# Folding the last two quarters of w_in through sums and differences of the weights' halves

## The chip, the cores and the metric

The kernel runs on one core of a Trainium2 chip. The metric is the device time of one execution in microseconds; lower is better. The engines are TensorE (PE, with its weight loads shown as PEld), VectorE (DVE), ScalarE (ACT), GpSimd (POOL) and the SyncE queue (SP), which issues all DMAs here.

## The reference

The input `x` is 8 batches of 3008 x 256 fp32. The reference takes the real part of a 2-D FFT over both axes of each batch, and sends the 24064 resulting rows through a feed-forward layer:

```
X = fft(fft(x, axis=1), axis=2).real          # rows of 256
h = X @ w_in                                  # w_in: 256 x 2048
g = h if h >= 1; 0 if h <= -1; else (h + 1)**2 / 4
out = g @ w_out                               # w_out: 2048 x 256
```

The weights arrive as 64-bit floats.

## The kernel before

The FFT over the 256 columns is never computed on the data. It is a matrix of cosines and sines, and is multiplied into `w_in` once ("the fold"). So the kernel has two kinds of work: the FFT over 3008 rows (as 47 x 64, two stages of fp32 matmuls, per batch), and for every unit two matrix products with a nonlinearity between.

**Units.** A unit is one batch, one chunk of up to 512 output columns (three chunks a batch) and one block of 128 of the 2048 hidden features. `gemm1` (G) makes two products u and v, each of three fp32r matmuls (high and low halves of the operands). VectorE makes `us` (U) and then both sums in `h` (H), ScalarE `a` (R, Q), VectorE the larger of both (L), ScalarE the high half `gh` (J), GpSimd the two low halves `gl` (T, t). `gemm2` (M) multiplies by `w_out`, twelve matmuls, four units behind G. The tile `h` has three buffers, so H of a unit needs GpSimd to be done with t of the unit three before; `uv` has three banks of PSUM, shared with the folds of quarters 2 and 3.

**Weights.** `w_in` and `w_out` come in sixteen jobs of 128 x 512 values. Jobs 8 and 9 are the upper and lower half (rows 0 to 127 and 128 to 255) of quarter 2 of `w_in`, 12 and 13 those of quarter 3. Step l loads a job's 64-bit words into a raw tile on SP, e and v turn them into fp32 on ScalarE and VectorE (v's last instruction is L238). The two halves of a quarter share a pair tile (`cv_8`, `cv_12`). From job 8 on, raw tiles and pair tiles lie in the four buffers of the tag `xt`, in which also the first four `x` tiles of batches 1 and on lie (steps X). A buffer goes to a new tile when every instruction that touches the old one has been done.

**The fold.** Step a (cosines) or b (sines) of a quarter multiplies the constant matrices `mats[m][h]` with the two fp32 halves and adds both products in one PSUM bank: `out = sum over h of mats[m][h].T @ half[h]`. An fp32 matmul leaves two records in the trace. Then a.1 and b.1 take the high part to `wh` on ScalarE (b.1 first copies row 0, which is sent by two DMAs to `delta`), a.2 and b.2 the low part to `wl` on VectorE, and b.2 clears row 0 with two GpSimd memsets.

**Order.** For the first batch and part of the second the order of PE, ACT, DVE and POOL is written out by hand in WRITTEN: each engine takes its own instructions in that order. SP is not in it. In WRITTEN, y1 adds the two halves of x tile 1 of batch 1 (loaded by X1) on GpSimd; its place is behind t17 and ahead of the clearing of b3.2, T18, t18, T19 and y0.

Of the kernel before, what the change touches and what calls it, by code (L numbers as in the profile page):

```python
# [9 lines left out]
F32 = mybir.dt.float32  # L10
# [3 lines left out]
ALU = mybir.AluOpType  # L14
# [8 lines left out]
NA, NBB, NC = 64, 47, 24  # L23
P = 128
XC = 8
GPC = 4
KT = 3
XW = KT * P
CH = 512
# [5 lines left out]
C_ORDER = [*range(1, 8), 0, *range(8, NC)]  # L35
WIDTH = [7 * NA + 34, CH, CH]

G_ORDER = np.arange(P).reshape(XC, GPC, 2, 2).transpose(0, 3, 1, 2).reshape(-1)


SPANS = [(k * P // NBB * 2 * NC, (min((k + 1) * P, 8 * NBB) - 1) // NBB * 2 * NC + 2 * NC) for k in range(KT)]
# [3 lines left out]
def _constants():  # L45
# [7 lines left out]
    rm = np.block([[co, si], [-si, co]])  # L53
    ang = 2 * np.pi * (np.outer(k, G_ORDER) % D) / D
    mc, ms = np.cos(ang), np.sin(ang)
# [22 lines left out]
t2 M2 G6.1 G7 o6 J4 p12.1 T3 l8 t3 M3 T4 t4 o6.1 H5 R5 l9 Q5 p12.2 G7.1 H6 G8 U7 G8.1 R6 e7 Q6 L5 J5 T5 t5 H7  # L78
R7 v7 o7 L6 U8 M4 p13 o7.1 M5 Q7 p13.1 p13.2 L7 J6 J7 T6 t6 T7 t7 H8 p14 p14.1 G9 G9.1 G10 U9 H9 G10.1 U10
p14.2 R8 Q8 R9 Q9 e8 H10 L8 L9 J8 T8 R10 M6 G11 M7 G11.1 G12 M7.1 U11 M7.2 v8 U12 G12.1 M7.3 M7.4 Q10 J9 t8 M8  # L80
e9 H11 L10 J10 G13 U13 G13.1 T9 t9 H12 M9 T10 t10 v9 H13 R11 R12 Q11 Q12 L11 L12 R13 G14 U14 b2 G14.1 M10 G15
J11 T11 t11 Q13 L13 M11 J12 b2.1 T12 t12 H14 U15 b2.2 l10 G15.1 G16 R14 J13 l13 Q14 T13 t13 H15 a2 G16.1 L14
U16 H16 a2.1 R15 J14 M12 Q15 L15 a2.2 R16 J15 e12 Q16 T14 t14 G17 U17 G17.1 H17 R17 Q17 M13 v12 e13 G18 X0 U18
G18.1 G19 T15 t15 L16 H18 R18 v13 X1 L17 M14 M15 M15.1 J16 T16 Q18 t16 U19 M15.2 b3 L18 G19.1 G20 M15.3 H19
M15.4 M16 J17 T17 t17 y1 J18 b3.1 b3.2 U20 G20.1 G21 a3 H20 G21.1 R19 Q19 L19 U21 M17 T18 t18 H21 X3 G22 G22.1
M18 R20 J19 Q20 L20 R21 a3.1 U22 a3.2 G23 J20 Q21 l11 T19 y0 t19 H22 T20 t20 X2 y2 G23.1 l15 G24 M19 M20 U23
L21 H23 e11 R22 J21 Q22 T21 t21 v11 R23 o11 Q23 G24.1 o11.1 l14 L22 J22 T22 t22 q0 G25 q0.1 U24 H24 G25.1 R24
G26 Q24 U25 e10 L23 J23 H25 M21 G26.1 G27 L24 v10 J24 R25 T23 t23 o10 e14 M22 M23 o10.1 T24 t24 Q25 U26 G27.1
# [19 lines left out]
N_EARLY = 8  # L108
# [20 lines left out]
def fft_ffn_kernel(ctx: ExitStack, tc: tile.TileContext, x, cst, w_in, w_out, out):  # L129
    nc = tc.nc  # L130
# [14 lines left out]
    def fold_x(b, q):  # L145

        t = xt.pop((b, q))
        if b or q:
            y = sb.tile([P, XW], F32, tag="y", name=f"y_{b}_{q}", bufs=3) if b else t[:, 0]
            nc.gpsimd.tensor_tensor(y, t[:, 0], t[:, 1], op=ALU.add)  # L150
            yt[b, q] = [y]
        else:
            yt[b, q] = [t[:, 0], t[:, 1]]
        if q == 0:
            y = sb.tile([P, NA], F32, tag="yd", name=f"yd_{b}", bufs=1)
            nc.gpsimd.tensor_tensor(y, t[:, 0, :NA], t[:, 1, :NA], op=ALU.subtract)
            yt[b, "d"] = y
# [5 lines left out]
    mats = [[cm[:, (2 * m + h) * P : (2 * m + h + 1) * P] for h in range(2)] for m in range(2)]  # L163
# [14 lines left out]
    def fft_bank(b, name):  # L178

        if b == 0 and early[0] < EARLY_BANKS:  # L180
            early[0] += 1
            return ps.tile([P, CH], F32, tag=f"acc{early[0] % 4}", name=name, bufs=1)
        return ps.tile([P, CH], F32, tag="fft", name=name, bufs=1)

    def split(hi, lo, src, eng=nc.vector):
        nc.scalar.activation(hi, src, AF.Copy)
        yield
        eng.tensor_tensor(lo, src, hi.bitcast(F32), op=ALU.subtract)  # L188
# [2 lines left out]
    jobs = []  # L191
    for f4 in range(4):
        jobs += [("in", f4, 0), ("in", f4, 1), ("out", 2 * f4), ("out", 2 * f4 + 1)]
    raws, mags, f32s, drows = {}, {}, {}, {}

    def load_w(n):
        if n >= len(jobs):
# [29 lines left out]

    def assemble(n):
        raw, t = raws.pop(n), mags.pop(n)
        low, high = raw[:, :, 0], raw[:, :, 1]  # L230
        bits = t.bitcast(U32)
        if n in VECTOR_LOWS:
            nc.vector.tensor_scalar(low, low, 2.0**-29, 7.0, op0=ALU.mult, op1=ALU.min)
        nc.vector.scalar_tensor_tensor(bits, bits, 3, low, op0=ALU.logical_shift_left, op1=ALU.bitwise_or)
        if n not in f32s:
            f32s[n] = low.bitcast(F32)
        w = f32s[n].bitcast(U32)
        nc.vector.scalar_tensor_tensor(w, high, 0x80000000, bits, op0=ALU.bitwise_and, op1=ALU.bitwise_or)  # L238
# [13 lines left out]
    def fold_bank(f4, name):  # L252
        if f4 < 2:
            return fft_bank(0, name)
        return ps.tile([P, CH], F32, tag="uv", name=name, bufs=3)

    def fold_w_in(f4, m):
        cols = slice(f4 * CH, (f4 + 1) * CH)
        pt = fold_bank(f4, f"wps_{f4}_{m}")
        for h in range(2):  # L260
            nc.tensor.matmul(pt, mats[m][h], f32s[4 * f4 + h], start=(h == 0), stop=(h == 1))  # L261
        yield
        if m == 0:
            yield from split(wh[m][:, cols], wl[m][:, cols], pt)
            return
        t = sb.tile([P, CH], F32, tag="us", name=f"drow_{f4}", bufs=2)[:1]
        nc.scalar.activation(t, pt[:1, :], AF.Copy)
        drows[f4] = t
        if f4:
            row = dr.tile([1, CH], F32, tag="drow", name=f"drow_{f4}", bufs=2)  # L270
            nc.sync.dma_start(row, t)
            nc.sync.dma_start(delta[:, f4 * 4 : f4 * 4 + 4], row.rearrange("o (i p) -> p (o i)", p=P))
        yield from split(wh[m][:, cols], wl[m][:, cols], pt)
        if f4:
            clear_row(f4)

    def clear_row(f4):
        for w in (wh, wl):
            nc.gpsimd.memset(w[1][:1, f4 * CH : (f4 + 1) * CH].bitcast(F32), 0.0)

    def first_delta():
        t = drows[0]
        pt = fft_bank(0, "dps")[:, : 4 * NA].rearrange("p (i n) -> p i n", i=4)
        for i in range(4):
            nc.tensor.matmul(pt[:, i], t[:, i * P : (i + 1) * P], half[:1].to_broadcast([1, NA]), start=True, stop=True)
        yield
        nc.scalar.activation(delta[:, :4], pt[:, :, 0], AF.Copy, scale=2.0)

    def stage1(b, q):
        for p in range(q, min(q + 2, XC)):  # L290
            if b > 1 and (b, p) not in yt:
                fold_x(b, p)
        if q == 0:
            zt[b] = sb.tile([P, NC, P + 1], F32, tag="z", name=f"z_{b}", bufs=1)
        z, y = zt[b], yt[b, q]
        bank = fft_bank(b, f"s1_{b}_{q}")
        pt = bank[:, : 8 * 2 * NC]
        for k, (lo, hi) in enumerate(SPANS):
            for j, part in enumerate(y):
                at = k, j  # L300
                mm = nc.tensor.matmul(  # L301
                    pt[:, lo:hi],
                    part[:, k * P : (k + 1) * P],
                    bm[:, BM[k] : BM[k + 1]],
                    start=at == (0, 0),
                    stop=at == (KT - 1, len(y) - 1),
                    skip_group_check=True,
                )
                if at == (0, 0):
                    pinned(b, mm)  # L310
        if q == 0:
            pd = bank[:NA, 8 * 2 * NC : 9 * 2 * NC]
            nc.tensor.matmul(pd, yt[b, "d"], bm[:, : 2 * NC], start=True, stop=True)
        yield
        for h in range(2):
            for m in range(2):
                src = pt[h * NA : (h + 1) * NA].rearrange("p (t m c) -> p m c t", t=8, m=2)[:, m]
                dst = z[m * NA : (m + 1) * NA, :, (2 * q + h) * 8 : (2 * q + h + 1) * 8]
                if b == 0 and q in VECTOR_COPIES:
                    nc.vector.tensor_copy(dst, src)  # L320
                else:
                    nc.scalar.activation(dst, src, AF.Copy)  # L322
        if q == 0:
            for m in range(2):
                nc.scalar.activation(z[m * NA : (m + 1) * NA, :, P], pd[:, m * NC : (m + 1) * NC], AF.Copy)
# [13 lines left out]
    def nyquist_spread():  # L339

        pt = fft_bank(0, "nys").rearrange("p (c d) -> p c d", d=NA)
        for c in range(8):
            lhs = zt[0][:, c, P : P + 1].to_broadcast([P, P])
            nc.tensor.matmul(pt[:, c], lhs, rm[:, :NA], start=True, stop=True)
        yield
        nyb[0, 0] = sb.tile([P, CH], F32, tag="nyb", name="nyb_0_0", bufs=4)
        nc.scalar.activation(nyb[0, 0].rearrange("p (c d) -> p c d", d=NA), pt, AF.Copy)
# [27 lines left out]
    def pinned(b, matmul):  # L375

        if b:
            tc.keep_in_program_order(matmul)

    def fft_pieces(b):  # L380
        pieces = []
        for q in range(XC):
            pieces.append(stage1(b, q))
        pieces.append(nyquist(b))
        for h in range(NC // 4):
            pieces.append(stage2(b, h))
        return pieces
# [6 lines left out]
    for b in range(NB):  # L394
        visits = 1 if b else 2
        m = NFT // visits
# [189 lines left out]
    def fill(n):  # L586
# [18 lines left out]
        "o": split_w_out,  # L605
        "m": lambda n: load_cm(),
        "a": lambda n: fold_w_in(n, 0),
        "b": lambda n: fold_w_in(n, 1),
        "w": fill,
        "n": lambda n: nyquist_spread(),  # L610
        "d": lambda n: first_delta(),
        "G": gemm1,
# [99 lines left out]
```

## Time and profile before

| | |
|---|---|
| median of 3 runs | 1721.83 us (1721.65 to 1722.29) |
| profiled execution, span from first to last instruction | 1720.0 us |
| time around the span (median less span) | 1.83 us |
| TensorE busy | 1708.5 us, 99% |
| VectorE, ScalarE, GpSimd busy | 80%, 79%, 70% |
| chain that ended last | PE 75%, POOL 11%, issue 5%, ACT 4%, DVE 4% |

A time in a row is in microseconds from the start of the span. A row of a timeline has a start, a duration, the engine, the line of the kernel and the operation, output before inputs; in brackets stands the idle time ahead of it and what ended it. Rows with "x4" are four instructions that followed each other. Matmul records overlap: a 512-column fp32r matmul shows some 0.39 us, and the next starts 0.23 us later.

### The profile page before, as it was taken

What the parts mean: (1) busy time and instruction counts of PE and PEld (TensorE: products, weight loads), DVE (VectorE), ACT (ScalarE), POOL (GpSimd) and SP (SyncE); (2) the same over time, 40 slices, a digit from 0 to 9 for tenths busy, and PEclk for the clock granted to TensorE, in tenths of its full rate; (3) what the DMA queues carried; (4) which work ended last, traced back from release to release, by engine and by line L of the source; (5) the groups of instructions that cost most, each with busy time, mean ns of one, the idle gap of its engine ahead of it and who ended that gap; (6) DMA issues with size and microseconds to landing.
All of it is one profiled execution on the core that took longest, in us unless ns stands there. A gap on an engine that the chain in (4) does not pass through costs nothing.

```text
span 1720.0 us, 21494 instructions
## 1 busy us (share of the span) xinstructions
PE 1708.5 (99%) x7782; PEld 1404.1 (82%) x7782; DVE 1384.2 (80%) x1683; ACT 1355.9 (79%) x1593; POOL 1197.4 (70%) x856
## 2 busy tenths in 40 slices
PE   9999999999999999999999999999999999999999
PEld 6878888888888888888888888888788888888776
DVE  6998888777888778887888778887788777888887
ACT  7878877878777877788877887778877788777776
POOL 3777766877667866768666786667766676766775
PEclk9999999999999999999999999999999999999999
DMA  6123320111001010011100111001100001000000
GB/s 234 48 74 119 101 70 25 52 37 53 19 7 60 28 53 25 10 51 38 44 25 10 51 46 35 26 10 60 50 21 26 10 24 43 1 25 24 1 26 25
DMA packets 33456, 72.44 MB, mean 42 GB/s; under 512 B 4547, under 2 KB 9667, under 8 KB 33350
## 3 DMA queue, kind: packets, MB, share of 16 engines
q1 hardware_dynamic: 33350, 71.07, 12.5%
q8 instruction: 61, 1.00, 0.3%
q14 instruction: 45, 0.37, 0.1%
HBM read 43.25 MB, written 27.81 MB: 41 GB/s over the span
## 4 chain that ended last, share of the span: by engine, by line
PE 75%; POOL 11%; issue 5%; ACT 4%; DVE 4%; DMA 0%; SPq 0%; POOLq 0%; ACTq 0%; DVEq 0%
PE acc L572 46%; PE uv L418 23%; POOL gl L471 9%; PE s L367 2%; PE s L301 2%; DVE h L462 2%; ACT gh L466 2%; ACT a L451 1%; POOL y L150 1%; ACT a L447 1%; DVE h L442 1%; DVE h L441 0%; DMA raw<-in_moe_w_in_dram 0%; DVE us L433 0%; PE wps L261 0%
## 5 line engine op out<-in xcount | busy, mean ns | idle before, releaser
L471 POOL TENSOR_TENSOR gl<-h,gh 128x512 fp32r<-128x512 f32 (+1 forms) x764 | 1094.6, 1456 | 487.8 <-ACT gh L466 441.4
L462 DVE SCALAR_TENSOR_TENSOR h<-a,h 128x1024 f32<-128x1024 f32 (+1 forms) x385 | 567.5, 1475 | 237.1 <-ACT a L451 236.6
L466 ACT ACTIVATE gh<-h 128x1024 fp32r<-128x1024 f32 (+1 forms) x385 | 400.6, 1041 | 310.4 <-DVE h L462 272.8
L572 PE MATMUL acc<-gh,woh 128*128 128x512 f32 (+1 forms) x1536 | 606.5, 395 | 0.0
L572 PE MATMUL acc<-gl,woh 128*128 128x512 f32 (+1 forms) x1536 | 601.8, 392 | 0.9 <-POOL gl L471 0.8
L572 PE MATMUL acc<-gh,wol 128*128 128x512 f32 (+1 forms) x1536 | 595.3, 388 | 0.0
L447 ACT ACTIVATE a<-h,half 128x1024 f32<-128x1024 f32 (+1 forms) x385 | 431.8, 1122 | 23.0 <-DVE h L442 20.1
L451 ACT ACTIVATE a<-a 128x1024 f32<-128x1024 f32 (+1 forms) x385 | 399.2, 1037 | 7.8
L572 PEld LDWEIGHTS acc<-gl,woh 128*128 128x128 f32 x1536 | 288.4, 188 | 62.6 <-POOL gl L471 1.9
L572 PEld LDWEIGHTS acc<-gh,wol 128*128 128x128 f32 x1536 | 289.2, 188 | 60.8 <-POOL wol L188 0.4
L572 PEld LDWEIGHTS acc<-gh,woh 128*128 128x128 f32 x1536 | 289.1, 188 | 55.9 <-DVE o L559 0.2
L441 DVE TENSOR_TENSOR h<-us,uv 128x512 f32<-128x512 f32 (+1 forms) x384 | 259.6, 676 | 64.4 <-POOL gl L471 23.6
L418 PE MATMUL uv<-pqh,wh 128*128 128x512 f32 (+1 forms) x768 | 305.9, 398 | 1.1 <-DVE h L442 0.9
L418 PE MATMUL uv<-pql,wh 128*128 128x512 f32 (+1 forms) x768 | 301.3, 392 | 0.0
L418 PE MATMUL uv<-pqh,wl 128*128 128x512 f32 (+1 forms) x768 | 298.6, 389 | 0.0
L433 DVE SCALAR_TENSOR_TENSOR us<-nyb,delta,uv 128x512 f32<-128x512 f32 (+1 forms) x384 | 278.7, 726 | 5.1 <-PE uv L418 4.5
L442 DVE TENSOR_TENSOR h<-us,uv 128x512 f32<-128x512 f32 (+1 forms) x384 | 256.2, 667 | 0.0
L418 PEld LDWEIGHTS uv<-pqh,wh 128*128 128x128 f32 x768 | 144.3, 188 | 38.8 <-DVE h L442 6.8
L418 PEld LDWEIGHTS uv<-pql,wh 128*128 128x128 f32 x768 | 144.3, 188 | 31.9
L418 PEld LDWEIGHTS uv<-pqh,wl 128*128 128x128 f32 x768 | 144.2, 188 | 31.0 <-issue 1.2
L322 ACT ACTIVATE z<-s 64x192 f32<-64x192 f32 x244 | 82.6, 339 | 4.4 <-PE s L301 0.7
L150 POOL TENSOR_TENSOR y<-x 128x384 f32<-128x384 f32 x56 | 80.7, 1443 | 0.7 <-PE s L301 0.7
(59 smaller groups left out, 493.8 us busy)
## 6 DMA issues: line engine op xcount, KB each, us to landing
x<-in_x_dram SPq DMA_DIRECT2D x64, 384.0 KB, 3.1
out_dram<-o SPq DMA_DIRECT2D x30, 512.0 KB, 3.2
out_dram<-o SPq DMA_DIRECT2D x16, 482.0 KB, 3.3
nyb<-nyr SPq DMA_DIRECT2D x23, 256.0 KB, 5.6
raw<-in_moe_w_in_dram SPq DMA_DIRECT2D x8, 512.0 KB, 8.5
raw<-in_moe_w_out_dram SPq DMA_DIRECT2D x8, 512.0 KB, 4.5
part<-o SPq DMA_DIRECT2D x4, 512.0 KB, 2.6
o<-part SPq DMA_DIRECT2D x4, 512.0 KB, 3.5
```

The costliest lines, as they stand in the source:

```text
L150: nc.gpsimd.tensor_tensor(y, t[:, 0], t[:, 1], op=ALU.add)
L322: nc.scalar.activation(dst, src, AF.Copy)
L418: nc.tensor.matmul(t[:, :n], w[m][:, cols], r[:, m, :n], start=(j == 0), stop=(j == 2))
L433: fixed(i, nc.vector.scalar_tensor_tensor(us, nyb[b, k][:, :n], d, uv[0], op0=ALU.mult, op1=ALU.add), 2)
L441: fixed(i, nc.vector.tensor_tensor(h[:, 0], us, v, op=ALU.subtract), 2)
L442: fixed(i, nc.vector.tensor_tensor(h[:, 1], us, v, op=ALU.add), 2)
L447: fixed(i, nc.scalar.activation(a[:, sl], h[:, sl], AF.Relu, bias=half, scale=0.5), 2)
L451: fixed(i, nc.scalar.activation(a[:, sl], a[:, sl], AF.Square), 2)
L462: fixed(i, nc.vector.scalar_tensor_tensor(h[:, sl], a[:, sl], 1.0, h[:, sl], op0=ALU.min, op1=ALU.max))
L466: fixed(i, nc.scalar.activation(gh[:, sl], h[:, sl], AF.Copy))
L471: fixed(i, eng.tensor_tensor(gl[:, sg], h[:, sg], gh[:, sg].bitcast(F32), op=ALU.subtract))
L572: nc.tensor.matmul(acc[:, :n], w[:, f, wc], g[:, sg], start=(first and j == 0), stop=(last and j == 2))
```

## The change

For even frequencies the constant matrix has the same values in its lower as in its upper half, for odd ones the negated values. So `G_ORDER`, the order of the 128 frequencies, now puts all 64 even ones first and the 64 odd ones last (before, they were in groups of 8), and for quarters 2 and 3 the fold is computed from the sum and the difference of the two halves: the even outputs from `lo + hi`, the odd ones from `lo - hi`, each with 64 of the 128 columns of one constant matrix, into the upper or lower 64 partitions of the same bank. A new step s makes the sum and the difference on GpSimd. The sum goes into the raw tile of the second job (9 or 13), the difference in place of the second half. In WRITTEN, s2 stands behind R11 (for GpSimd: behind t10 and ahead of T11), s3 behind t16 and ahead of T17, and b3 goes from ahead of G19.1 to behind G20. The FFT's first stage writes its copies into `z` in the new order. Quarters 0 and 1 fold as before.

```diff
-G_ORDER = np.arange(P).reshape(XC, GPC, 2, 2).transpose(0, 3, 1, 2).reshape(-1)
+G_ORDER = np.arange(P).reshape(XC, GPC, 2, 2).transpose(3, 0, 1, 2).reshape(-1)
...
-... v9 H13 R11 R12 Q11 Q12 L11 L12 R13 G14 U14 b2 G14.1 M10 G15
+... v9 H13 R11 s2 R12 Q11 Q12 L11 L12 R13 G14 U14 b2 G14.1 M10 G15
...
-... X1 L17 M14 M15 M15.1 J16 T16 Q18 t16 U19 M15.2 b3 L18 G19.1 G20 M15.3 H19 M15.4 M16 J17 T17 t17 y1
+... X1 L17 M14 M15 M15.1 J16 T16 Q18 t16 s3 U19 M15.2 L18 G19.1 G20 M15.3 H19 M15.4 b3 M16 J17 T17 t17 y1
...
     def assemble(n):
         raw, t = raws.pop(n), mags.pop(n)
+        if n >= N_EARLY:
+            spent[n] = raw
...
         for h in range(2):
-            nc.tensor.matmul(pt, mats[m][h], f32s[4 * f4 + h], start=(h == 0), stop=(h == 1))
+            if f4 < 2:
+                nc.tensor.matmul(pt, mats[m][h], f32s[4 * f4 + h], start=(h == 0), stop=(h == 1))
+            else:
+                g = slice(h * P // 2, (h + 1) * P // 2)
+                nc.tensor.matmul(pt[g], mats[m][0][:, g], sums[f4][h], start=True, stop=True)
...
+    def sum_w_in(f4):
+        lo, hi = f32s[4 * f4], f32s[4 * f4 + 1]
+        total = spent.pop(4 * f4 + 1).rearrange("p e two -> p (e two)")[:, :CH].bitcast(F32)
+        nc.gpsimd.tensor_tensor(total, lo, hi, op=ALU.add)
+        nc.gpsimd.tensor_tensor(hi, lo, hi, op=ALU.subtract)
+        sums[f4] = total, hi
...
-                dst = z[m * NA : (m + 1) * NA, :, (2 * q + h) * 8 : (2 * q + h + 1) * 8]
+                dst = z[m * NA : (m + 1) * NA, :, (XC * h + q) * 8 : (XC * h + q + 1) * 8]
...
+        "s": sum_w_in,
```

## Rows read from the trace of the kernel before

**Rows 1.** The page's first part: busy time of each engine.

```profile
PE 1708.5 (99%) x7782; PEld 1404.1 (82%) x7782; DVE 1384.2 (80%) x1683; ACT 1355.9 (79%) x1593; POOL 1197.4 (70%) x856
```

**Rows 2.** Windows: length, then busy PE, PEld, DVE, ACT, POOL, clock, DMA.

```profile
100.00:113.00 13.00, 13.00 (x55) 9.87 (x53) 12.80 (x17) 11.39 (x15) 7.30 (x6) 1.00 0.30 102
127.00:230.00 103.00, 101.47 (x463) 82.71 (x463) 89.31 (x111) 89.30 (x117) 79.87 (x60) 1.00 0.35 113
...
400.00:1700.00 1300.00, 1298.85 (x5926) 1074.37 (x5925) 1040.96 (x1248) 1018.89 (x1162) 908.51 (x637) 1.00 0.09 29
```

**Rows 3.** Chain of waits, end of the stretch 80 to 130: start, length, what.

```profile
125.19 1.27 POOL gl L471
...
126.48 0.69 DVE h L441
...
127.82 0.93 PE uv L418 x3
```

**Rows 4.** Timeline of PE: folds b2, b3, M16's first matmul, fold a3.

```profile
81.81 1.88 PE L261 MATMUL wps<-cv,cm 128*128 128x512 f32 x4
...
109.42 1.88 PE L261 MATMUL wps<-cv,cm 128*128 128x512 f32 x4
...
112.54 0.39 PE L572 MATMUL acc<-gh,woh 128*128 128x512 f32 x1
...
116.70 1.88 PE L261 MATMUL wps<-cv,cm 128*128 128x512 f32 x4
```

**Rows 5.** The folds' tile: durations in ns, minimum, median, maximum.

```profile
L261 PE MATMUL wps<-cv,cm x32: 590/592/697, 11.5 to 118.0; 128*128 128x512 f32 x32
```

**Rows 6.** Timeline of POOL: T10 t10, T11 on, T16 t16, y1, T18 t18, T19.

```profile
78.70 2.56 POOL L471 TENSOR_TENSOR gl<-h,gh 128x512 fp32r<-128x512 f32 x2
85.09 6.05 POOL L471 TENSOR_TENSOR gl<-h,gh 128x512 fp32r<-128x512 f32 x4 [3.83 <-ACT gh L466]
...
108.82 2.64 POOL L471 TENSOR_TENSOR gl<-h,gh 128x512 fp32r<-128x512 f32 x2 [5.41 <-ACT gh L466]
...
114.91 1.03 POOL L150 TENSOR_TENSOR y<-x 128x384 f32<-128x384 f32 x1
...
116.81 2.51 POOL L471 TENSOR_TENSOR gl<-h,gh 128x512 fp32r<-128x512 f32 x2
121.64 1.29 POOL L471 TENSOR_TENSOR gl<-h,gh 128x512 fp32r<-128x512 f32 x1 [2.32 <-ACT gh L466]
```

**Rows 7.** Timeline of DVE: v9's end, L11 L12, L16, L18, H21's first.

```profile
80.59 0.69 DVE L238 SCALAR_TENSOR_TENSOR cv<-raw,cps 128x512 uint32<-128x512 uint32 x1
...
82.50 2.35 DVE L462 SCALAR_TENSOR_TENSOR h<-a,h 128x1024 f32<-128x1024 f32 x2
...
104.20 1.22 DVE L462 SCALAR_TENSOR_TENSOR h<-a,h 128x1024 f32<-128x1024 f32 x1
...
110.25 2.29 DVE L462 SCALAR_TENSOR_TENSOR h<-a,h 128x1024 f32<-128x1024 f32 x1
...
121.20 0.69 DVE L441 TENSOR_TENSOR h<-us,uv 128x512 f32<-128x512 f32 x1
```

**Rows 8.** Timeline of SP: the loads l13 and X1.

```profile
81.34 0.33 SPq L206 DMA_DIRECT2D raw<-in_moe_w_in_dram  x1
...
108.02 0.33 SPq L142 DMA_DIRECT2D x<-in_x_dram  x1
```

**Rows 9.** Waits of SP, 103 to 109.5: us in total, times, longest.

```profile
SPq L142 <- DVE cv L238: 18.6, 2, 14.7
```

**Rows 10.** The page's part 6: DMA issues, last number us to landing.

```profile
x<-in_x_dram SPq DMA_DIRECT2D x64, 384.0 KB, 3.1
...
raw<-in_moe_w_in_dram SPq DMA_DIRECT2D x8, 512.0 KB, 8.5
```

**Rows 11.** Timeline of ACT: e13's first instruction, J16.

```profile
104.88 0.62 ACT L223 ACTIVATE cps<-raw 128x512 f32<-128x512 f32 x1
...
107.70 1.04 ACT L466 ACTIVATE gh<-h 128x1024 fp32r<-128x1024 f32 x1
```

More of the change, by code (lines that the diff above doesn't have):

```diff
@@ L80 @@
 p14.2 R8 Q8 R9 Q9 e8 H10 L8 L9 J8 T8 R10 M6 G11 M7 G11.1 G12 M7.1 U11 M7.2 v8 U12 G12.1 M7.3 M7.4 Q10 J9 t8 M8
-e9 H11 L10 J10 G13 U13 G13.1 T9 t9 H12 M9 T10 t10 v9 H13 R11 R12 Q11 Q12 L11 L12 R13 G14 U14 b2 G14.1 M10 G15
+e9 H11 L10 J10 G13 U13 G13.1 T9 t9 H12 M9 T10 t10 v9 H13 R11 s2 R12 Q11 Q12 L11 L12 R13 G14 U14 b2 G14.1 M10 G15
 J11 T11 t11 Q13 L13 M11 J12 b2.1 T12 t12 H14 U15 b2.2 l10 G15.1 G16 R14 J13 l13 Q14 T13 t13 H15 a2 G16.1 L14
 U16 H16 a2.1 R15 J14 M12 Q15 L15 a2.2 R16 J15 e12 Q16 T14 t14 G17 U17 G17.1 H17 R17 Q17 M13 v12 e13 G18 X0 U18
-G18.1 G19 T15 t15 L16 H18 R18 v13 X1 L17 M14 M15 M15.1 J16 T16 Q18 t16 U19 M15.2 b3 L18 G19.1 G20 M15.3 H19
-M15.4 M16 J17 T17 t17 y1 J18 b3.1 b3.2 U20 G20.1 G21 a3 H20 G21.1 R19 Q19 L19 U21 M17 T18 t18 H21 X3 G22 G22.1
+G18.1 G19 T15 t15 L16 H18 R18 v13 X1 L17 M14 M15 M15.1 J16 T16 Q18 t16 s3 U19 M15.2 L18 G19.1 G20 M15.3 H19
+M15.4 b3 M16 J17 T17 t17 y1 J18 b3.1 b3.2 U20 G20.1 G21 a3 H20 G21.1 R19 Q19 L19 U21 M17 T18 t18 H21 X3 G22 G22.1
 M18 R20 J19 Q20 L20 R21 a3.1 U22 a3.2 G23 J20 Q21 l11 T19 y0 t19 H22 T20 t20 X2 y2 G23.1 l15 G24 M19 M20 U23
@@ L193, in fft_ffn_kernel @@
         jobs += [("in", f4, 0), ("in", f4, 1), ("out", 2 * f4), ("out", 2 * f4 + 1)]
-    raws, mags, f32s, drows = {}, {}, {}, {}
+    raws, mags, f32s, drows, spent = {}, {}, {}, {}, {}
     def load_w(n):
@@ L275, in fold_w_in @@
             clear_row(f4)
+    sums = {}
+    def sum_w_in(f4):
[4 more added lines that the diff above has]
+        sums[f4] = total, hi
     def clear_row(f4):
```

## The prediction, made before the result was known

> **What bounds the kernel now.** I read the page's engine totals first: TensorE is busy for 1708.5 of 1720.0 us [rows 1]. Then the windows: from 127 to 230 us it is idle for 103.00 - 101.47 = 1.53 us, from 400 to 1700 us for 1.15 us [rows 2]. So time that TensorE loses before 127 us has almost nowhere to be won back. All that the change touches stands between 78 and 128 us, where the order is written out by hand. So next I read the chain of waits there [rows 3]: it does not run over TensorE. It goes over GpSimd's `gl` subtractions to VectorE's `h` (the `h` tile of three units ago must have been read by GpSimd) and only from there to TensorE: t19 ends at 126.46, H22 follows at 126.48, G24 at 127.82. In this stretch GpSimd and VectorE hold the line, and TensorE meets it at 127.82 with no slack. Last I read the queues of the engines step by step [rows 4 to 11].
>
> The run's time has a median of 1721.83 us and the profiled execution a span of 1720.0 us [rows 1]; the 1.83 us around the span I leave as they are, and add the sum to the median.
>
> **TensorE's part.** A fold is two fp32 matmuls, each two records, the four together 1.88 us with the last one's 0.592 [rows 4, 5], so 0.43 from one to the next, and 4 x 0.43 = 1.72 us of TensorE's queue. The four changed folds (b2, a2, b3, a3) still have four records of 512 columns, at half the width. No row shows two half-width matmuls beside each other, so I bound it: one after the other, nothing is saved; wholly side by side, a fold takes 0.86. The records come in order: pass 1 and pass 2 of the first matmul, then both of the second. Only the first's pass 2 and the second's pass 1 are neighbours in different halves, so I take 3 x 0.43 = 1.29: 0.43 saved each, 1.7 in all, 3.4 at most.
>
> The Trainium skill, TensorEngine Tiling (Array Packing), Key Properties and Theoretical Speedup, says that column tiles of 64 load and multiply in parallel and independently, up to twice as fast. By it alone a fold would take 0.86 us and the sum below would end 0.43 lower, since only a3's length stands on the path. No run so far shows the pair; I hold to the record order.
>
> The copies into `z` keep shape and stride: nothing. The constants are reordered on the host: nothing.
>
> **The sums on GpSimd.** Each of s2 and s3 adds two subtractions or additions of 128x512 f32. The nearest row has the same size: T10 and t10 together 2.56, so 1.30 each with a little overlap [rows 6]. VectorE's L462 and GpSimd exclude each other: alone L462 takes 1.22, but 2.29 where it came just after t16 had begun (t16 ends 108.82 + 2.64 = 111.46, L18 ends 112.54) [rows 6, 7].
>
> *s2, b2.* t10 ends at 78.70 + 2.56 = 81.26, v9 at 80.59 + 0.69 = 81.28 [rows 6, 7]. First sum 81.35 to 82.65. At 82.50 two L462 come back to back (2.35) [rows 7]. I let one go ahead, to 83.85, then the second sum to 85.15, then L12. If both sums go first the second ends at 83.95; if both L462, at 86.35. TensorE reaches b2 at 81.81 [rows 4]; its second matmul can start at 85.2 and takes 0.86: 86.05 instead of 81.81 + 1.72 = 83.53, so 2.5 late (1.4 to 3.7). This hits the chain once more: L12 ends at 86.3 and T11, ready at 85.09 [rows 6], goes behind it, so t11 comes 1.3 later, and with it H14, whose `h` tile t11 frees. VectorE's work from 100 to 113 is dense (12.80 of 13.00) [rows 2], and I carry these 1.3 us to t16 (0 to 2.5).
>
> *s3, b3.* b3 moves on TensorE past G19.1 and G20, six matmuls of 0.23: arrival at 109.42 + 1.39 = 110.8 instead of 109.42 [rows 4]. Its other steps (the drow copy with its two DMAs, the split, the clearing) stay in place. But s3 stands on GpSimd behind T16 and t16, which wait until 108.82 for J16 (107.70 + 1.04) [rows 6, 11]. t16 ends at 111.46, plus 1.3 is 112.8; the waiting L18 goes first (to 113.9), the sums end at 115.1 and 116.4, and b3's second matmul runs to 117.25. M16 behind it began at 112.54 [rows 4]: TensorE is now 4.7 late. If the sums beat L18, it is 3.5; without the carried 1.3, 3.4. ScalarE's b3.1 waits too, with R19 and Q19 behind it; these are done by about 120, before anything needs them.
>
> **The buffers: the largest term.** The sum is put into the raw tile of job 9 or 13, so this `xt` slot is free after the folds, not after the assembly. There are four slots. Before, load l13 went out at 81.34 and X1 at 108.02, in each case just after an assembly: the SP queue's waits put 18.6 us of L142's two waits on the assembly's last instruction (L238) [rows 8, 9]. At 108 the other three slots hold raw_10 (until o10), X0 (until y0) and cv_12 (until a3). So X1 must now wait for a3.
>
> l13 waits for a2 instead, until about 96; even with the 8.5 us median of such loads [rows 10] it lands at 104.5, and e13 ran at 104.88 [rows 11], now some 1.3 later: hidden, with under 2 us to spare. On SP the two `part` stores, drow and delta may stand behind X1 until 123; their readers are units of the second visit, from unit 24 on: hidden. l11 and X3 go out by about 127.3, and their readers on ScalarE and GpSimd stand behind the same delay: hidden.
>
> y1 can't be hidden: it adds X1's halves on GpSimd, and T18, t18, T19, y0 and t19 are queued behind it. From M16 to a3 it is 116.70 - 112.54 = 4.16 us [rows 4]: a3 starts at 121.4, and ends, at 1.29 + 0.16 for the tail of its last record (592 - 430 ns), at 122.85. X1 goes out at about 123.0 and lands 3.1 later (median of 64) [rows 10]: 126.1. y1 and two clearings to T18's start took 116.81 - 114.91 = 1.90, T18 and t18 2.51 [rows 6]: t18 ends at 130.5. J19 is there by then, so T19 to t19's end follow at once, 126.46 - 121.64 = 4.82 [rows 3, 6]: 135.3. H22 and G24 stand on t19: 135.3 - 126.46 = 8.9 us late. TensorE itself, 4.3 late after a3, would get there earlier and waits (already for H21, which needs t18).
>
> **Sum.** +8.9 at G24. From there GpSimd, VectorE and TensorE are late by the same amount, so I take nothing back; at most 1.5 of it goes into TensorE's idle time up to 230 us [rows 2]. 1721.83 + 8.9 = 1730.7. Own range: without s2's 1.3 and with 1.5 absorbed +6; both L462 first, X1 slowed by another transfer and y1 by an L462 +12: 1728 to 1734.
>
> **Rivals.**
> 1. *X1 has another slot.* For it: nothing that I see in the rows; against it: X1's and l13's release so far. Then only the sums count: T17 and t17 follow s3 at 116.4, t18 ends at about 123.4, and TensorE's own 4.7 - 0.4 at a3, less 0.3 waited at G24, is the later: +4.0, 1725.8 (+2 to +5).
> 2. *Not slower: the lag of four units swallows it.* GpSimd has idle time ahead of T11 (3.83), T16 (5.41) and T19 (2.32) [rows 6], and gemm2 runs four units behind gemm1. Place: H21, which in the trace came 1.9 after t18 (119.32, against 121.20) [rows 6, 7]. Price: the folds' 1.7 come through, 1720.1. It decides if t18 is less than 1.9 us late; by the rows it is 11 late, since the idle time lies ahead of the T's and the sums behind them.
> 3. *The change does not save on TensorE*: the halves run one after the other. Then a3 ends 0.43 later: 1731.1, inside the first range. The opposite, all four folds halved and no wait anywhere, gives 1721.83 - 3.44 = 1718.4.
>
> **How the numbers follow.** Forecast, with or without rival 3's serial halves: 0.62. Rival 1: 0.20. Rival 2, or waits that just eat the gain: 0.14. All halved and nothing waits: 0.04. A measurement of this kernel tells 0.2%, 3.4 us, from no change. Slower by more: the 0.62 and some two thirds of rival 1, 0.75; within: the rest of it and rival 2, 0.21; faster: 0.04. The range takes in the forecast and rival 1, 1722.5 to 1734, and leaves about 0.14 below and 0.05 above.
>
> **What would show it.** On SP the X1 load issued right after a3's last matmul, and y1 on GpSimd waiting for that DMA; TensorE idle ahead of b2's and b3's second half for GpSimd; VectorE's H21 waiting for t18 far longer; the four folds 1.29 long. If X1 still goes out right after v13, rival 1 is true. If the sums of s3 end before 110.8, the step on b3 is wrong, and if TensorE's idle time after 127 us shrinks by more than 1.5 us, so is my carrying the whole lag to the end.

## The result, and the profile after

The changed kernel takes 1734.55 us (median of five runs, 1732.36 to 1735.19), the kernel before in the same rounds 1721.83 (1721.47 to 1723.69): 1.0069 times as long, 95% interval [1.0057, 1.0081]. The profiled execution has a span of 1731.7 and a time of 1733.66 us. The forecast of 1730.7 has the right side and lies some 4 us too low; the time is 0.55 us above 1734, where both of its ranges end.

First the page's engine totals of the changed kernel, then its windows (length, busy PE, PEld, DVE, ACT, POOL with counts, clock, DMA share, GB/s) in the two later stretches of [rows 2]:

```profile
PE 1712.2 (99%) x7782; PEld 1404.5 (81%) x7782; DVE 1385.3 (80%) x1683; ACT 1355.9 (78%) x1593; POOL 1203.3 (69%) x860
```

```profile
127.00:230.00 103.00, 97.32 (x429) 79.23 (x428) 83.45 (x100) 83.66 (x110) 79.05 (x64) 0.97 0.31 101
400.00:1700.00 1300.00, 1299.22 (x5931) 1075.34 (x5930) 1042.07 (x1248) 1021.56 (x1168) 911.14 (x638) 1.00 0.09 30
```

GpSimd has four instructions and 5.9 us more than in [rows 1]. From 400 us on little differs: TensorE idles for 0.78 us, against 1.15 before. From 127 to 230 TensorE now idles 103.00 - 97.32 = 5.68 us, against 1.53 in [rows 2], and its mean granted clock is 0.97, where it was 1.00. Of these 5.68 us, 4.61 are one wait ahead of G22.1 (shown below). So the lag arises before and shortly after 127 us and is never made good.

The chain of waits from 110 to 142 us (start, length, what) shows where:

```profile
112.31 2.22 POOL raw L288
...
114.61 1.27 POOL cv L289
115.88 2.45 POOL gl L486 x2
118.33 8.16 issue
...
128.46 2.46 POOL gl L486 x2
...
130.94 0.69 DVE h L456
...
132.28 1.65 PE uv L433 x3
133.92 4.87 PE acc L587 x12
```

It runs over the sums of s3, then stands 8.16 us, then over y1, T18 and t18 to H21, and then, unlike in [rows 3], over TensorE itself. The standing time is the load of X1, as SP's timeline (l13, then X1 with X3 behind it) and its waits from 80 to 142 us show, where [rows 9] named VectorE's assembly:

```profile
95.38 0.34 SPq L206 DMA_DIRECT2D raw<-in_moe_w_in_dram  x1
...
123.36 0.81 SPq L142 DMA_DIRECT2D x<-in_x_dram  x2
```

```profile
SPq L142 <- PE wps L267: 3.3, 1, 3.3
SPq L206 <- PE wps L267: 6.4, 1, 6.4
```

GpSimd's timeline, answering [rows 6]: s2's sums, T16 and t16, s3's sums, T17 and t17, y1.

```profile
81.15 1.28 POOL L288 TENSOR_TENSOR raw<-cv 128x512 f32<-128x512 f32 x1
82.52 2.14 POOL L289 TENSOR_TENSOR cv<-cv 128x512 f32<-128x512 f32 x1
...
109.65 2.66 POOL L486 TENSOR_TENSOR gl<-h,gh 128x512 fp32r<-128x512 f32 x2 [5.40 <-ACT gh L481]
112.28 2.25 POOL L288 TENSOR_TENSOR raw<-cv 128x512 f32<-128x512 f32 x1
114.61 1.27 POOL L289 TENSOR_TENSOR cv<-cv 128x512 f32<-128x512 f32 x1
115.83 2.50 POOL L486 TENSOR_TENSOR gl<-h,gh 128x512 fp32r<-128x512 f32 x2
126.53 1.02 POOL L150 TENSOR_TENSOR y<-x 128x384 f32<-128x384 f32 x1 [8.19 <-DMA x<-in_x_dram]
```

TensorE's timeline, answering [rows 4]: b2; a2 between its neighbours; b3 and M16; from G22.1 to G24.

```profile
82.49 1.07 PE L267 MATMUL wps<-raw,cm 128*64 128x512 f32 x2 [0.73 <-POOL raw L288]
84.70 1.07 PE L267 MATMUL wps<-cv,cm 128*64 128x512 f32 x2 [1.14 <-POOL cv L289]
...
93.91 0.40 PE L433 MATMUL uv<-pql,wh 128*128 128x512 f32 x1
94.24 0.64 PE L267 MATMUL wps<-raw,cm 128*64 128x512 f32 x1
94.24 0.64 PE L267 MATMUL wps<-cv,cm 128*64 128x512 f32 x1
94.72 0.59 PE L267 MATMUL wps<-raw,cm 128*64 128x512 f32 x1
94.72 0.59 PE L267 MATMUL wps<-cv,cm 128*64 128x512 f32 x1
...
95.58 0.39 PE L433 MATMUL uv<-pqh,wl 128*128 128x512 f32 x1
...
114.58 1.97 PE L267 MATMUL wps<-raw,cm 128*64 128x512 f32 x2 [2.40 <-POOL raw L288]
115.93 1.97 PE L267 MATMUL wps<-cv,cm 128*64 128x512 f32 x2
117.83 0.51 PE L587 MATMUL acc<-gh,woh 128*128 128x512 f32 x1
...
132.28 0.79 PE L433 MATMUL uv<-pqh,wh 128*128 128x512 f32 x1 [4.61 <-DVE h L457]
132.87 0.63 PE L433 MATMUL uv<-pqh,wl 128*128 128x512 f32 x1
133.30 0.63 PE L433 MATMUL uv<-pql,wh 128*128 128x512 f32 x1
...
140.03 0.39 PE L433 MATMUL uv<-pqh,wh 128*128 128x482 f32 x1
```

G24 starts at 140.03 instead of 127.82, 12.2 us late. Behind the wait of 4.61 us ahead of G22.1 the matmuls follow each other at 0.43 us instead of 0.23. The windows of the changed kernel, columns as above, give the clock to it:

```profile
112.00:118.00 6.00, 3.60 (x6) 0.74 (x6) 3.19 (x4) 1.54 (x3) 5.92 (x5) 0.72 0.40 164
...
132.00:139.00 7.00, 6.72 (x17) 5.29 (x18) 6.16 (x6) 4.83 (x7) 4.68 (x6) 0.55 0.20 56
```

In the last stretch the granted clock is 0.55, between the levels of 1.2 (0.50) and 2.4 GHz (1.00), nearly all of it at the lower one.

### The profile page after: what moved, and what is told of

Same layout as the page of the kernel before. It is cut to its first block, busy times and chain, and to the rows that moved or that the text cites. A ratio compares the mean times of both kernels' runs of the same rounds, so it can differ in the third digit from the quotient of the medians.

```text
span 1731.7 us, 21506 instructions
## 1 busy us (share of the span) xinstructions
PE 1712.2 (99%) x7782; PEld 1404.5 (81%) x7782; DVE 1385.3 (80%) x1683; ACT 1355.9 (78%) x1593; POOL 1203.3 (69%) x860
## 4 chain that ended last, share of the span: by engine, by line
PE 81%; POOL 5%; ACT 5%; DVE 4%; issue 4%; DMA 0%; SPq 0%; ACTq 0%; POOLq 0%; DVEq 0%
PE acc L587 50%; PE uv L433 25%; POOL gl L486 4%; DVE h L477 3%; PE s L316 2%; PE s L382 2%; ACT gh L481 2%; ACT a L466 2%; ACT a L462 1%; POOL y L150 1%; DVE h L457 0%; DMA raw<-in_moe_w_in_dram 0%; DVE h L456 0%; DVE us L448 0%; ACT z L337 0%
```

## The experiments

This table shows, for each profile, how much later an instruction comes than in the profile of before, whose times stand in the first line (in us; starts, but ends for t16, t18 and the span). The ratio is the timed one to before, with its 95% interval.

| kernel | t16 | M16 | t18 | H21 | G22.1 | G24 | span | ratio |
|---|---|---|---|---|---|---|---|---|
| before, at | 111.46 | 112.54 | 119.32 | 121.20 | 122.58 | 127.82 | 1720.0 | |
| changed | 0.85 | 5.30 | 11.58 | 9.74 | 9.70 | 12.21 | 11.7 | 1.0069 [1.0057, 1.0081] |
| e1, y1 later | 1.48 | 5.83 | 4.48 | 5.01 | 6.23 | 5.86 | 5.2 | 1.0023 [1.0014, 1.0033] |
| e2, own tile | 2.58 | 7.01 | 5.67 | 5.67 | 6.63 | 6.26 | 5.1 | 1.0022 [1.0013, 1.0031] |
| e3, tile held | 0.07 | 0.10 | 6.04 | 4.20 | 4.16 | 5.43 | 4.5 | 1.0024 [1.0014, 1.0034] |
| e4, TensorE kept busy | 1.36 | 4.90 | 11.23 | 9.38 | 9.71 | 10.05 | 8.2 | 1.0056 [1.0044, 1.0069] |
| e5, no sums | 0.27 | -0.43 | 0.30 | 0.30 | 0.26 | 0.29 | 0.5 | 0.9996 [0.9987, 1.0005] |
| e6, b2 later | 1.38 | 4.91 | 3.95 | 3.95 | 4.52 | 4.14 | 5.3 | 1.0023 [1.0014, 1.0032] |
| e7, b2 and b3 later | 0.88 | -0.92 | 3.43 | 3.43 | 3.39 | 3.41 | 4.5 | 1.0020 [1.0011, 1.0029] |
| e8, e7 with y1 later | 0.77 | -1.02 | 3.27 | 3.27 | 3.23 | 3.25 | 4.8 | 1.0016 [1.0007, 1.0025] |
| e9, s3 earlier | 3.90 | 0.62 | 2.93 | 2.93 | 2.89 | 2.90 | 4.2 | 1.0017 [1.0008, 1.0026] |
| e10, changed again | 0.96 | 4.50 | 10.61 | 8.76 | 8.72 | 11.18 | 10.4 | 1.0063 [1.0050, 1.0075] |
| e11, e4 again | 0.94 | 4.48 | 10.81 | 8.97 | 9.28 | 9.63 | 8.9 | 1.0053 [1.0040, 1.0065] |

### The buffer: e1, e2, e3

Theory: the sum's stay in the raw tile makes X1 late, and y1, which waits for X1 on GpSimd, carries this to TensorE. Rival: the sums' time and TensorE's waits do it, and X1 only happens to be late too. The wait was removed in two ways. e1 leaves the tile as it is and moves y1, and X3 with it, behind t19:

```diff
-... T17 t17 y1 J18 ... T18 t18 H21 X3 G22 ... T19 y0 t19 H22 ...
+... T17 t17 J18 ... T18 t18 H21 G22 ... T19 y0 t19 y1 X3 H22 ...
```

> The changed kernel, with y1 (GpSimd's addition of the x tile that X1 loads) moved in the written order from behind t17 to behind t19, and the load X3 behind it; the sum still lies in the raw tile, so X1 still goes out only after a3. Theory (the largest term is y1, queued ahead of T18, waiting for X1): t18 ends at about 121 to 124 instead of 130.9, VectorE's H21 and TensorE's G22.1 do not wait for it, and TensorE keeps its full clock after it; what is left are the waits of b2 and b3 for the sums, TensorE being some 5 us late at M16 less 0.5 at a3: 4 to 5 us above before (1726 to 1727). Rival (the sums on GpSimd cost it all, and y1 stands in time that is lost anyway): unchanged, 10 to 13 us above before.

e2 leaves the order as it is and gives the sum a tile of its own, so that the raw tiles are free after the assembly again:

```diff
-        total = spent.pop(4 * f4 + 1).rearrange("p e two -> p (e two)")[:, :CH].bitcast(F32)
+        total = sb.tile([P, 2, CH], F32, tag="pqh", name=f"total_{f4}", bufs=4)[:, 0]
```

> The changed kernel in its own order, but the sum is written to a tile of its own (a free buffer of the tag pqh) instead of the raw tile, so the raw buffers are free after the assembly as before. Theory: l13 and X1 go out at about 81 and 109 again, y1 does not wait; left are the waits of b2 and b3 for the sums: 4 to 5 us above before, as with y1 moved. Rival (the sums cost it all): 10 to 13 us above. If this one is faster than y1 moved, the later load l13 costs something too.

Both take two thirds of the loss away, to 1.0023 and 1.0022 (3.9 and 4.0 us by the medians, at the lower end of the 4 to 5 expected). In e1 y1 now comes long after X1 has landed; T18 and t18 stand ahead of it, from 121.28. In e2 SP's timeline has l13 at its place of [rows 8] again, and X1 is there when y1 comes (120.01, no wait):

```profile
81.34 0.34 SPq L206 DMA_DIRECT2D raw<-in_moe_w_in_dram  x1
```

e3 is the opposite test: the kernel before, without any sum, in which job 13 alone is assembled in its raw tile, so that this slot is held until a3:

```diff
-        if n < N_SBUF or jobs[n][0] == "in":
+        if n < N_SBUF or jobs[n][0] == "in" and n != 13:
```

> The kernel before, with no sums and full-width folds, but job 13's fp32 values are assembled in its raw tile (every second word) instead of the pair tile, so that this raw buffer is held until a3, as in the change. Theory (the buffer's lifetime): X1 goes out at about 118.7 after a3, lands at 122, t18 ends at about 126.5 instead of 119.3, G22.1 comes 5.4 us late, and if TensorE's clock falls in that wait as in the changed kernel, another 2 to 3 us: 5 to 8 us above before. Rival (sums alone): no difference, within 1 us.

The held tile alone makes the kernel slower, 1.0024, with M16 on time (+0.10). That is 4.1 us by the medians; 5 to 8 were expected. In its profile TensorE's clock does fall after the wait, and the lag grows from 4.16 at G22.1 to 5.43 at G24. X1 goes out at 117.88, not 108.02, y1 waits for it, and TensorE for t18 by way of H21 (GpSimd's and TensorE's timelines):

```profile
120.98 1.02 POOL L150 TENSOR_TENSOR y<-x 128x384 f32<-128x384 f32 x1 [5.95 <-DMA x<-in_x_dram]
```

```profile
126.74 0.80 PE L418 MATMUL uv<-pqh,wh 128*128 128x512 f32 x1 [3.80 <-DVE h L442]
```

So the buffer is a cause by itself. In the changed kernel it costs more: X1, which stands on a3, goes out 5.5 us later there than in e3.

### The clock: e4, and e10 with e11

Theory: of the loss some 3 to 4 us are TensorE's lower clock after its waits. Rival: GpSimd's lag sets it all, and what the lower clock costs falls into waits. e4 fills the waits ahead of b3 and G22.1 with matmuls whose result nobody reads:

```diff
+    def keep_busy(n):
+        for _ in range(n):
+            nc.tensor.matmul(fft_bank(1, "busy"), cs[:, :P], cs[:, :CH], start=True, stop=True)
...
-... M15.4 b3 M16 ... H21 X3 G22 G22.1 ...
+... M15.4 W2 b3 M16 ... H21 X3 G22 W5 G22.1 ...
```

> The changed kernel with idle matmuls on constants put into TensorE's two long waits: two fp32 matmuls of 512 columns ahead of b3, five ahead of G22.1, whose results nothing reads. Theory (some 3 to 4 us of the loss are TensorE running at half its clock after it stood still): records after G22.1 come 0.23 us apart instead of 0.43, b3 ends about 1 us earlier, and the time falls to 7 to 9 us above before. Rival (the waiting chain through t18 and H21 sets the end, the clock costs nothing): unchanged at 11 to 13 us, or more by what the added matmuls take.

e4's windows, columns as above:

```profile
112.00:118.00 6.00, 5.32 (x14) 1.76 (x13) 3.69 (x4) 2.44 (x3) 5.92 (x5) 1.00 0.43 175
...
132.00:139.00 7.00, 6.88 (x28) 4.89 (x28) 7.00 (x7) 5.08 (x7) 4.68 (x5) 1.00 0.21 56
```

The clock is 1.00 in both, t18 and G22.1 come about as late as in the changed kernel (+11.23 and +9.71, there +11.58 and +9.70), but from G22.1 to G24 the lag grows by 0.34 us, not by 2.51. The time is 10.4 us above before by the medians, where the theory had 7 to 9, and the ratio of 1.0056 does not stand clear of 1.0069. So both kernels were run again together, unchanged.

> The changed kernel once more, beside the next run on the same chip. All theories: 11 to 13 us above before.

> The changed kernel with the idle matmuls ahead of b3 and G22.1, on the same chip as the change itself. Theory (TensorE's lower clock after its two long waits is 2 to 3 us of the loss): 2 to 3 us below the change. Rival (the chain through t18 and H21 alone): the same as the change.

The window 132 to 139 of e10, then of e11, and e11's timeline of TensorE:

```profile
132.00:139.00 7.00, 7.00 (x21) 5.49 (x20) 5.67 (x6) 5.10 (x7) 4.69 (x6) 0.62 0.20 56
```

```profile
132.00:139.00 7.00, 6.87 (x29) 5.02 (x29) 7.00 (x7) 5.09 (x7) 4.68 (x6) 1.00 0.19 56
```

```profile
126.67 5.75 PE L607 MATMUL busy<-cs 128*128 128x512 f32 x10
...
132.50 0.39 PE L433 MATMUL uv<-pqh,wl 128*128 128x512 f32 x1
132.73 0.40 PE L433 MATMUL uv<-pql,wh 128*128 128x512 f32 x1
```

From G22.1 to G24 the lag grows by 2.46 us at 0.62 and by 0.35 at 1.00. So the traces show, twice, about 2.1 us for the clock (2.51 - 0.34, 2.46 - 0.35). The changed kernel is 10.1 us above before this time, not 11 to 13. The times of the two differ in the direction of the theory, by less than the 2 to 3 us expected: 1.05 us between the medians. The ratios to before, 1.0063 and 1.0053, have intervals that overlap, but all five runs of e11 (1730.06 to 1731.67) lie below all five of e10 (1731.83 to 1734.35). So the timing shows a gain; its size is told by the traces only.

### What is left without the buffer: e5 to e9

With e2's tile 0.2% stay. Theory after e2: this is TensorE, which waits at b2 and b3. Rival: GpSimd, whose queue is longer by four instructions. e5 keeps e2's order and the half-width folds, but leaves the sums out (the folds take the halves as they are):

```diff
-        total = sb.tile([P, 2, CH], F32, tag="pqh", name=f"total_{f4}", bufs=4)[:, 0]
-        nc.gpsimd.tensor_tensor(total, lo, hi, op=ALU.add)
-        nc.gpsimd.tensor_tensor(hi, lo, hi, op=ALU.subtract)
-        sums[f4] = total, hi
+        sums[f4] = lo, hi
```

> The changed kernel in its own order with the four half-width folds, but without the sums: the folds take the two halves as they are, so s2 and s3 issue nothing and their part of the result is left out; the raw buffers are free as before. What the half-width folds alone are worth. Theory (side by side, a fold takes 1.21 us instead of 1.72, and TensorE's place in this stretch is set by others): 0 to 2 us below before. If every saved microsecond of TensorE counted, 2.0 below; if b3's later place costs something, at or above before.

0.9996: what remains is the sums, and the folds' shorter time brings nothing that can be measured even with no sums to pay for. TensorE comes earlier to the places behind the folds (M16 -0.43) and waits more there. Its weight loads' waits for `h` from 78 to 128 us (total, times, longest), in before and then in e5:

```profile
PEld uv L418 <- DVE h L442: 1.5, 3, 0.7
```

```profile
PEld uv L428 <- DVE h L452: 4.4, 5, 1.0
```

e6 and e7 keep the sums, with e2's tile, and take TensorE's waits away: e6 moves b2 behind M10, e7 also b3 behind M16 (and R19, Q19 ahead of ScalarE's b3.1).

```diff
-... G14 U14 b2 G14.1 M10 G15 ...
+... G14 U14 G14.1 M10 b2 G15 ...
```

> The sum in a tile of its own, and b2 moved on TensorE from ahead of G14.1 to behind M10, so that it comes when both sums of s2 are done; everything else as changed. Tells the two waits for the sums apart. Theory (b2's wait costs TensorE 2.0 us, but most of the final lag is set by b3's wait): 2.5 to 4 us above before, against 4.0 with only the tile. Rival (both waits add up): 2 us above before.

```diff
-... M15.4 b3 M16 J17 ... J18 b3.1 b3.2 ... R19 Q19 L19 ...
+... M15.4 M16 b3 J17 ... J18 R19 Q19 b3.1 b3.2 ... L19 ...
```

> As with b2 moved, and b3 moved behind M16, with R19 and Q19 ahead of b3.1 on ScalarE. Theory: TensorE waits only about 1 us for the second sum of s3, saves 0.5 at each fold, and GpSimd comes 1 to 3 us late to T19: -1 to +1.5 us against before, no difference that can be told. Rival (GpSimd is the line, so it does not help to move TensorE's part): still 3 to 4 us above before.

e6 changes nothing in the time (1.0023 against e2's 1.0022; 4.3 us by the medians, where 2.5 to 4 were expected and 2 by the rival): no cost of TensorE's wait at b2 can be told from the times. In e7 M16 comes 0.92 us *earlier* than in before, and yet G24 is 3.41 late and the time 1.0020. So the theory (-1 to +1.5 us) fell and the rival (3 to 4 us) holds: 3.4 us by the medians. GpSimd's timeline in e7 shows its way: t16, the sums of s3, T17 and t17, without a gap. At the end of that way VectorE's H22, on which G24 stands, waits for t19, as in [rows 3] (VectorE's timeline, last line).

```profile
109.67 2.67 POOL L483 TENSOR_TENSOR gl<-h,gh 128x512 fp32r<-128x512 f32 x2 [5.41 <-ACT gh L478]
112.31 2.25 POOL L285 TENSOR_TENSOR total<-cv 128x512 f32<-128x512 f32 x1
114.64 1.29 POOL L286 TENSOR_TENSOR cv<-cv 128x512 f32<-128x512 f32 x1
115.89 2.51 POOL L483 TENSOR_TENSOR gl<-h,gh 128x512 fp32r<-128x512 f32 x2
```

```profile
129.89 0.69 DVE L453 TENSOR_TENSOR h<-us,uv 128x512 f32<-128x512 f32 x1 [1.18 <-POOL gl L483]
```

e8 is e7 with e1's move of y1 and X3:

> As the one before, with y1 and the load X3 also moved behind t19, so that GpSimd has 1 us less ahead of T18. Theory (GpSimd is the line from T17 to t19): 0.5 to 1 us below the one before, -1.5 to +0.5 against before. Rival (TensorE is the line): the same as the one before.

Nothing more comes of it that can be told (1.0016; G24 3.25 against 3.41): with the sum in its own tile, y1 holds nobody up by more than that. e9 tries to put s3's sums into GpSimd's idle time ahead of T16, with v13 behind t15, s3 behind it and J16 ahead of R18:

```diff
-... R17 Q17 M13 v12 e13 G18 ... T15 t15 L16 H18 R18 v13 X1 L17 ... M15.1 J16 T16 Q18 t16 s3 U19 ...
+... R17 M13 v12 e13 Q17 G18 ... T15 t15 v13 s3 X1 L16 H18 J16 R18 L17 ... M15.1 T16 Q18 t16 U19 ...
```

> The sum in its own tile, b2 behind M10, and s3 put into GpSimd's idle stretch ahead of T16 instead of behind t16: v13 goes ahead of L16 on VectorE, e13 ahead of Q17 and J16 ahead of R18 on ScalarE, b3 stays behind G20. The sums and their number are the same. Theory (GpSimd's queue from T17 to t19 is the line, and 2.6 of the 3.4 us that both sums cost come from s3 standing ahead of T17): T17 and t17 end within 1.5 us of before, and the time is 0 to 1.5 us above before. Rival (the sums cost their 2.6 us wherever they stand, or the moved assembly costs as much): 3 us or more above before.

GpSimd's timeline in e9:

```profile
107.42 2.15 POOL L285 TENSOR_TENSOR total<-cv 128x512 f32<-128x512 f32 x1 [3.15 <-DVE cv L237]
109.65 2.24 POOL L286 TENSOR_TENSOR cv<-cv 128x512 f32<-128x512 f32 x1
111.85 6.01 POOL L483 TENSOR_TENSOR gl<-h,gh 128x512 fp32r<-128x512 f32 x4
```

v13 does not end before 107.3, so 3.15 of the idle time pass unused; the sums take 4.4 us here, push t16 back by 3.90, and 2.90 are left at G24. The time is 2.9 us above before, so the theory (0 to 1.5) fell here too. No version that was run beats the kernel before. By e5, whose interval goes down to 0.9987, one that merely hid the sums would have 2 us to win at most.

## Why the forecast was right in its side and 4 us low

- **The buffers**, called the largest term: right. X1 went out at 123.36 (forecast 123.0), l13 at 95.38 (96), y1 started at 126.53 (126.1), t18 ended at 130.91 (130.5). e1 and e2 remove the term, e3 makes it alone. Rival 1, that X1 has another slot, is out for the changed kernel; its +4.0 is what e2 gives, timed +0.22%, 3.8 us.
- **s2 and b2.** The second sum ended at 84.66 (85.15), t16 0.85 late (1.3). TensorE's 2.5 us there were not in the sum, and by e6 rightly: the times show no cost of them.
- **s3 and b3.** M16 was 5.30 late (4.7). The order came as forecast: L18 went first, the first sum took 2.25, the second 1.27. The sums ended even 0.5 sooner than forecast (115.88, not 116.4). What was short is b3's second matmul: from 115.93 to M16 at 117.83 are 1.90 us at the lower clock, against 0.86 forecast. In e10, the same program, the clock there was full, the same way took 1.01 us and M16 was 4.50 late. By e7 what counts of this step is GpSimd's time, not TensorE's: t16 is 0.88 late, t18 3.43, so s2 carries 0.9 and s3 2.5 of it.
- **Rival 2**, the lag of four units swallows it: false. Even the 3.4 us of the sums alone came through (e7), and e9 shows why the idle time ahead of T16 does not help: with v13 moved ahead, the sums could still not start before it ended, at 107.3. The 1.9 us between t18 and H21, where this rival looked for slack, gave none in e7 either: both came 3.43 late.
- **TensorE's part.** My reading of the record order was wrong. In a2 the first passes of both matmuls start at 94.24 and the second ones at 94.72. From the `uv` matmul at 93.91 to the second one behind, at 95.58, are 1.67 us; less two intervals of 0.23 this leaves 1.21 for the fold, where I took 1.29. The rule that I set against it, in the Trainium skill, TensorEngine Tiling (Array Packing), Key Properties, is that different tiles can load weights and multiply in parallel. This trace agrees: the two column tiles go side by side, pass by pass, 0.48 apart. The 0.86 that I had by that rule was not reached: 1.21 - 2 x 0.48 = 0.25 us went ahead of, between and behind the passes. Rival 3 in its serial form is false; its other form needs the waits gone, and e5, which has no sums, is not faster.
- **The step that failed** is in the sum: "TensorE itself, 4.3 late after a3, would get there earlier and waits (already for H21, which needs t18)." It was early only up to G22.1. t19 ended 8.18 late, somewhat better than the 8.9 forecast, and no longer decides; G24 is reached by TensorE from H21 on, 9.70 late at G22.1, and then 2.5 more at the lower clock. I had followed GpSimd's chain past H21 and never TensorE's own queue of 127.82 - 122.58 = 5.24 us from G22.1 to G24, nor its clock, which in [rows 2] was 1.00 throughout. The wrong path alone was worth little: with t18 at 130.5, as forecast, H21 and G22.1 would have been 9.3 late, 0.4 above the sum. Another 0.4 is t18's, and 2.5 the lag that grew behind G22.1, 2.1 of it the clock by e4 and e11. So the term that the sum lacked is that a long wait costs more than its length. The upper end of my own range, +12, is near the 12.2 at G24 by luck: it stood there for other reasons, none of which occurred.
- **The lag carried to the end**: right. 12.2 at G24, 11.7 at the end of the span.

The 12.2 us at G24, by differences between profiles: 3.4 are the sums on GpSimd (e7). Some 6.4 go with X1's lateness (changed less e1), of which 2.1 are the clock. The rest, about 2.4, is e1 less e7: TensorE's waits at b2 and b3, and a lower clock behind b3 in e1's profile (0.89 from 112 to 118). In the times e1, e2, e6 and e7 do not differ, so I do not count it as shown. By the times alone, the sums cost 3.4 to 4.3 us (medians of e7 and e6), and the rest of the 12.7 (10.1 in e10's rounds), some 6 to 9 us, goes with the held buffer and the clock behind its wait. Alone the held tile costs 4.1 us (e3); there a3 is not late.

## What to carry to other kernels

A result that is put "for free" into a spent tile prolongs that tile's life: look up who takes the slot next, and whose queue waits for that load. When an engine's wait is forecast, follow each queue past it, TensorE's own too, and price the matmuls behind a long wait at the lower clock. Work taken off TensorE brought nothing in this stretch, where a subtraction on GpSimd ends last (e5), and work put on GpSimd there cost what its idle time did not take: 0.9 us of the 3.5 that s2 occupied, 2.5 of s3's 3.6 (e7).

## What the runs showed of the hardware

- After 4.61 us without a matmul TensorE ran at 0.43 us from one to the next until 138.40, where they again came 0.23 apart; granted clock 0.55 from 132 to 139, nearly all of it at the lower level of 1.2 GHz. In e10 it was the same after 4.44 us (0.62 from 132 to 139), in e3 after 3.80 us (0.66 from 126 to 131). Idle matmuls in the wait kept it at 1.00, twice.
- After shorter waits it was not the same each time. At b3 it was 0.72 from 112 to 118 after 2.40 us in the changed kernel's profile, but 1.00 after 2.40 us in e10, the same program, and 1.00 after 2.82 us in e6. At b2 e2 lost it after waits of 0.73 and 1.14 us about one fold matmul (0.76 from 84 to 91), and the changed kernel, with the same two waits, did not (1.00). Why, these runs do not tell.
- An fp32 pair of half-width matmuls ran pass by pass side by side, 1.21 us for a fold of 1.72.
